# Placing every load by the plan, writing key features over the exponentials, and searching the order of a transformer block anew

## The chip, the cores and the metric

The kernel runs on one core of a Trainium2 chip. Times are device microseconds (us) of that core. Runs come in a fast and, now and then, a slow state (a lower granted TensorE clock or a time over 1.5% above the fastest of its kernel); fast runs are compared with fast runs. PE is TensorE, PEld its weight loads, DVE VectorE, ACT ScalarE, POOL GpSimd, SP the engine that issues most DMAs. "KVZ" below is the moment at which the key/value state of the linear attention is written to SBUF; S is the sum over key exponentials of one 128-token tile. Other names of tiles in the lines below: xn are normalized tokens, raw the same tokens transposed by a DMA, hT the transposed tokens after the modulation (scale and shift, the columns modA and modB); e and eq are the exponentials of keys and queries, S and Sq their sums, R and Rq the reciprocals, phik the normalized key features, va the values, pT the transposed query features, wo_sb the output weights. "Fillers" are matmuls on ones that compute nothing and stand where the plan believes PE idle.

## The reference, cut to what matters

```python
def _A_ref(x, wqkv, w_phi, wo):            # linear attention, 32 heads of 16
    q, k, v = split(x @ wqkv)
    pq, pk = q @ w_phi, k @ w_phi          # per head
    phi_q = concat([softmax(pq), softmax(-pq)]); phi_k = concat([softmax(pk), softmax(-pk)])
    kv = einsum('bhsf,bhsd->bhfd', phi_k, v); z = phi_k.sum(s)
    return (phi_q @ kv) / (phi_q @ z + 1e-06) @ wo
# 2048 tokens of 512, silu(c) @ w_mod gives shifts, scales and gates
h = layernorm(x) * (1 + ca) + sa;  x = x + ga * _A_ref(h, ...)
h = layernorm(x) * (1 + cb) + sb;  x = x + gb * ((silu(h @ w_gate) * (h @ w_up)) @ w_down)   # 1376 wide
```

All tokens' keys and values go into `kv` before the first query can be answered. So the kernel has a stage that ends with KVZ, and one of attention output and feed-forward behind it.

## The kernel before: the parts concerned

The kernel describes its work as operations, each with the engines that may do it and a duration for each, and a long list ORDER that says in which sequence a greedy plan places them: an entry divided by four is the operation, the rest is the chosen engine. Only the sequence on each engine, the tile chosen for each buffer and the filler matmuls come out of the plan; the chip then runs with semaphores.

```python
HOP = {"PE": 0.24, "DVE": 0.2, "ACT": 0.2, "POOL": 0.14, ...}     # us to another engine
...
for x in ORDER:
    o = self.ops[x // 4]; o.alt = o.alts[x % 4]; o.eng = o.alt[0].rstrip("*")
    o.start = max([o.at, free[o.eng]] + [p.end + ... for p in o.preds])
    if o.alt[0] == "DVE*":                       # takes turns with GpSimd
        o.start = max(o.start, free["POOL"])
    for b in o.news:
        t, b.slot = self.room(b, live); o.start = max(o.start, t)
    o.end = free[o.eng] = o.start + o.alt[1]
    if o.alt[0] == "DVE*":
        free["POOL"] = max(free["POOL"], o.end)
...
for o in sorted(self.ops, key=lambda o: (o.start, o.n)):
    if o.eng == "PE":
        fill(last, o, fns)                       # matmuls on ones where PE is planned idle
```

The first nine loads stood outside the plan, in a fixed sequence, and a key tile went through this (line numbers of the profile in comments):

```python
load("x0", ...); load("wk", ...); load("phi", ...); load("m0", ...); load("m2", ...)
load("x2", ...); load("wv", ...); load("x4", ...); load("wq", ...)
...
e = sb("kph", "e", [P, G, 2, 4, DH], BF16)                                       # 3 tiles
pl.op("ACT", r=[pk], w=[e], ...)                                                 # L600, exp(+), exp(-)
pl.op("DVE", r=[e], w=[Ss], us=1.14, fn=... tensor_reduce)                       # L610, S
pl.op([("DVE", 0.46, reciprocal), ("ACT", 0.52, Ln then Exp)], r=[Ss], w=[R])    # L616 or L614/L615
bphik[i] = sb("kph", "phik", [P, G, 2, 4, DH], BF16)                             # 4 tiles
pl.op("POOL", r=[e, R], w=[bphik[i]], us=1.92, fn=... tensor_tensor mult)        # L618
# query tile
pl.op([("DVE", 0.12, Rq * Sq), ("POOL", 0.15, same)], ...)                       # L659 or L660
pl.op([("POOL", 1.0, eq * Rq), ("DVE", 0.62, same)], ...)                        # L664
```

The two kinds of query product (L659, L664) were not marked `DVE*` when placed on DVE; the modulation of transposed tokens (L558) was.

The softmax here doesn't subtract the row's maximum and nothing guards it: scores larger than these inputs give would overflow.

Of the kernel before, what the change touches and what calls it, by code (L numbers as in the profile page):

```python
# [14 lines left out]
P = 128  # L15
S = 2048
# [19 lines left out]
def fm_size(m):  # L36
# [11 lines left out]
    0, 348, 4, 72, 76, 32, 352, 24, 336, 300, 324, 12, 312, 36, 28, 104, 8, 41, 20, 16, 44, 109, 88, 52, 1220, 152, 156, 56, 93, 112, 160, 164, 168,  # L48
    49, 172, 180, 60, 120, 128, 96, 124, 132, 177, 80, 116, 64, 184, 372, 68, 136, 140, 212, 100, 204, 84, 216, 260, 145, 456, 150, 188, 376, 460,
    208, 192, 196, 364, 448, 252, 201, 221, 476, 264, 256, 408, 224, 360, 484, 269, 340, 392, 368, 380, 272, 416, 452, 480, 304, 400, 234, 230, 356,  # L50
    412, 508, 244, 308, 249, 282, 278, 385, 328, 516, 344, 316, 332, 396, 236, 488, 420, 320, 388, 292, 464, 404, 712, 425, 468, 472, 284, 540, 240,
    504, 716, 492, 288, 428, 297, 512, 692, 496, 520, 728, 433, 832, 576, 684, 912, 524, 720, 536, 438, 736, 445, 500, 780, 688, 844, 772, 836, 442,
    696, 868, 840, 872, 700, 740, 784, 876, 880, 732, 529, 724, 768, 704, 804, 776, 788, 580, 532, 708, 584, 744, 748, 812, 808, 917, 800, 904, 936,
    864, 792, 753, 1216, 852, 816, 856, 1172, 860, 764, 756, 820, 849, 884, 908, 796, 888, 1080, 544, 1144, 548, 1236, 1184, 761, 824, 828, 932,
    920, 1112, 1176, 1084, 552, 1088, 925, 1240, 928, 1152, 1148, 1108, 1228, 1140, 892, 648, 1096, 1100, 1180, 1189, 1200, 1116, 1120, 1092, 1196,
    1160, 1104, 1156, 1164, 1193, 612, 1128, 1232, 1168, 556, 1132, 1244, 1404, 560, 1248, 1124, 1136, 1252, 1224, 1204, 1408, 620, 1468, 616, 1472,
    1420, 1425, 1436, 1428, 565, 1412, 1416, 1440, 1484, 1489, 1256, 1432, 1208, 588, 1500, 1452, 1492, 592, 1464, 1444, 1508, 1448, 1504, 1496,
    1457, 1460, 1476, 1516, 656, 652, 1212, 1521, 1524, 1368, 624, 568, 572, 596, 1640, 1480, 896, 628, 601, 633, 1528, 1372, 1680, 660, 944, 1692,
    1512, 664, 1376, 1644, 900, 1260, 1696, 940, 1700, 1704, 1568, 1572, 1724, 604, 637, 1684, 1676, 608, 1648, 668, 1008, 972, 1264, 1688, 1728,
    1732, 640, 948, 1736, 1880, 1884, 672, 952, 1268, 1012, 644, 1604, 1740, 1888, 1744, 957, 1892, 980, 1576, 2032, 1612, 1532, 1608, 1896, 1296,  # L60
    1748, 1016, 680, 2036, 976, 1900, 1540, 676, 960, 1304, 1752, 2040, 1044, 1536, 1756, 1760, 2044, 984, 1300, 1904, 1764, 1332, 1776, 1052, 1048,
    1768, 988, 964, 1780, 968, 1908, 1336, 2184, 993, 996, 1773, 2188, 2048, 1912, 2192, 1844, 1788, 2052, 1916, 1020, 1340, 1840, 1784, 1848, 1922,
    1824, 2056, 1024, 1029, 2336, 1804, 1832, 1932, 1000, 1792, 1936, 1924, 1852, 1808, 2196, 1796, 1928, 1812, 2060, 1004, 1800, 2064, 2340, 1820,
    1940, 2344, 2348, 2069, 1056, 1944, 1816, 2360, 1992, 1060, 1996, 2352, 1828, 1948, 2200, 1032, 2204, 2356, 1856, 2072, 1836, 2364, 1860, 2208,
    1040, 1956, 1065, 2000, 2090, 2077, 2086, 2081, 2092, 2096, 1068, 2368, 1964, 2212, 2216, 1272, 2372, 2222, 1308, 1276, 2144, 1281, 1036, 1284,
    2148, 2608, 2388, 2612, 1076, 2004, 2376, 1072, 1864, 2152, 2224, 1976, 2616, 2380, 2392, 2386, 2396, 2156, 1312, 1984, 1288, 2108, 2400, 1292,
    2404, 2237, 2242, 2234, 2408, 2100, 2128, 2229, 2620, 1972, 2632, 1980, 2416, 1960, 1317, 1988, 2244, 2624, 1868, 2628, 2136, 2296, 1968, 1380,
    2413, 2248, 2300, 2880, 1320, 2884, 2124, 1384, 2304, 2420, 1616, 1620, 2116, 1388, 2280, 2636, 2308, 2276, 1625, 2252, 1328, 1544, 2008, 2132,
    2434, 2888, 1324, 2437, 2012, 2430, 2640, 2644, 2426, 1392, 1709, 2284, 2456, 2288, 1952, 1548, 2440, 2648, 2260, 2140, 2892, 2896, 2444, 2268,
    2652, 2112, 2120, 1553, 2660, 2524, 2448, 1396, 2532, 2016, 1720, 2292, 2664, 1400, 2657, 2160, 2544, 2900, 1344, 2104, 2460, 1628, 3164, 2904,  # L70
    2548, 2668, 1636, 2020, 2672, 1348, 2164, 2024, 3168, 2464, 2168, 2676, 2680, 1632, 3172, 1580, 2552, 2556, 2492, 2908, 1584, 2686, 2472, 3696,
    2264, 2480, 2688, 1589, 2912, 1353, 1593, 2692, 2272, 2705, 2701, 2932, 1356, 2709, 1556, 2508, 2500, 2916, 1364, 2698, 2488, 2496, 2172, 1360,
    2920, 2476, 3700, 3704, 2924, 1564, 2712, 2504, 2728, 2936, 2940, 2516, 2312, 1560, 2944, 2930, 2716, 3152, 2732, 2316, 3156, 2948, 2720, 3160,
    2256, 2512, 2952, 2764, 2960, 3424, 2760, 1652, 2958, 2964, 2520, 1656, 2528, 2320, 2768, 2536, 2800, 1660, 2540, 3204, 2981, 2736, 2973, 2452,
    2484, 2977, 3428, 2324, 2772, 2560, 2564, 2968, 1873, 3000, 1665, 2984, 1600, 3432, 3208, 1596, 3176, 2568, 2748, 3212, 2572, 2744, 3216, 3220,
    1668, 2988, 2329, 2752, 3436, 2780, 1672, 2808, 3720, 3224, 2788, 2756, 3440, 2796, 3448, 2468, 3444, 3180, 3004, 3008, 3229, 2804, 3184, 2584,
    3188, 3708, 3192, 3196, 3201, 2816, 2776, 2588, 3724, 3712, 2820, 2812, 3476, 3716, 2824, 3728, 3732, 3736, 3740, 3745, 2592, 3236, 3452, 3232,
    3254, 2028, 3456, 2828, 3460, 3748, 3464, 3246, 2784, 2740, 3032, 3241, 2792, 3480, 3036, 3484, 3249, 2332, 3488, 3492, 3040, 3256, 3272, 3044,
    2856, 3752, 3260, 2596, 3756, 2724, 3276, 3468, 3496, 3760, 2860, 3473, 2832, 3764, 3504, 3768, 3264, 3501, 3280, 2864, 3508, 3521, 3088, 3772,
    2601, 3776, 3524, 3516, 2992, 3513, 3092, 2836, 2868, 1717, 3528, 3096, 3544, 3780, 3548, 3532, 3284, 2577, 2840, 2996, 3785, 2844, 3789, 3100,  # L80
    3794, 1876, 2604, 3536, 3068, 3016, 3798, 3552, 3048, 3800, 2177, 3816, 3024, 3072, 3076, 3080, 3056, 1712, 3020, 3084, 3012, 3820, 3052, 3028,
    3344, 3804, 3128, 3268, 3060, 3064, 3132, 3136, 3104, 3108, 3808, 3112, 3308, 3324, 3140, 3352, 3332, 2873, 3304, 3340, 3824, 3348, 3288, 3296,
    2180, 3145, 3328, 3356, 3292, 3300, 3336, 3316, 3360, 3312, 3364, 3320, 3368, 3372, 3376, 3380, 3384, 2580, 3400, 3404, 3408, 3412, 3417, 3540,
    3420, 2849, 3560, 3148, 3116, 3616, 3828, 3576, 3584, 3624, 3612, 3600, 3568, 3636, 2852, 3580, 3564, 3620, 3588, 3572, 3596, 3604, 3592, 3632,
    3672, 3121, 3556, 3628, 3608, 3648, 3676, 3640, 3644, 3680, 3652, 3656, 3832, 3884, 3660, 3892, 3852, 3888, 3848, 3388, 3896, 3860, 3900, 3868,
    3836, 3904, 3840, 3872, 3812, 3856, 3665, 3864, 2876, 3392, 3684, 3844, 3396, 3908, 3912, 3876, 3880, 3920, 3916, 3688, 3924, 3124, 3692, 3928,
    3932, 3937, 3944, 3948, 3952, 3956, 3668, 3940, 3961, 3964, 3968, 3972, 3976, 3980, 3984,
# [35 lines left out]
class Plan:  # L123


    HOP = {"PE": 0.24, "DVE": 0.2, "ACT": 0.2, "POOL": 0.14, "SP": 0.0, "XBAR": 0.0, "NONE": 0.0}
    OWN = {"PE": 0.0, "DVE": 0.19, "ACT": 0.19, "POOL": 0.12, "SP": 0.0, "XBAR": 0.0, "NONE": 0.0}
    DMA = (1.8, 350e3, 0.6)

    def __init__(self, slots):  # L130
        self.ops = []
        self.slots = slots
        self.queue = 0.0, 0.0
# [34 lines left out]
    def run(self, fill):  # L168
        free = {e: 0.0 for e in self.OWN}
        live = {t: {} for t in self.slots}  # L170
        free["XBAR"], dma = self.queue
        for x in ORDER:
# [4 lines left out]
            if o.alt[0] == "DVE*":  # L177
                o.start = max(o.start, free["POOL"])
            for b in o.news:
                t, b.slot = self.room(b, live)  # L180
                o.start = max(o.start, t)
# [5 lines left out]
            if o.eng == "XBAR" and o.kb > 0:  # L187
                dma = max(dma, o.start + self.DMA[0]) + o.kb * 1024 / self.DMA[1]
                o.end = max(o.end, dma + self.DMA[2])
            elif o.eng == "XBAR" and o.kb == 0:  # L190
                dma = max(dma, o.end + 0.65) + 0.5
                o.end = max(o.end, dma + 0.05)
# [10 lines left out]
def kernel(  # L203
# [72 lines left out]
    pools["modp"] = modp  # L276

    lastf = fm_size(FM - 1)
    at = {}

    def load(name, dst, src, kb):
        nc.sync.dma_start(dst, src)  # L282
        sent[0] += kb
        at[name] = 2.1 + sent[0] * 1024 / 360e3 + 1.1
# [416 lines left out]
    for c_i in (2, 3):  # L701
        later(x_ch[c_i][:], x_v[c_i], bx[c_i * TPC:(c_i + 1) * TPC], 512)
# [329 lines left out]
```

## Time and profile before

| | before |
|---|---|
| median of 3 runs (215.97 with the fourth, taken later) | 216.40 us (215.53 to 216.98) |
| profiled span | 213.3 us, clock 1.000 |
| first S, KVZ, first gate matmul of the feed-forward | 17.0, 62.6, 74.5 us |
| DVE busy in the stretch from 17.0 to 62.5 | 44.70 of 45.50 us |
| PE idle behind KVZ | 6.3 us |

The moments are read from the timelines of DVE and PE: the start of the first reduction at L610, of the product that writes KVZ (L742), and of the first matmul at L853.

### The profile page before, as it was taken

The numbers are of one execution on the slowest core, as the hardware profiler recorded it, in microseconds if no ns is written. First come the engines' busy times: TensorE is split into PE (matmuls) and PEld (weight loads), VectorE is DVE, ScalarE is ACT, GpSimd is POOL, SyncE is SP. The second block draws the span as 40 slices with busy tenths as digits, with TensorE's granted clock in tenths as the row PEclk, the third lists the DMA queues.
The fourth block names the chain that finished last, engine by engine and source line by source line (L and its number), as shares of the span: only waits on it lengthen the run. The fifth ranks groups of instructions, "written<-read, shape, count | busy, mean of one in ns | idle before, by whom it ended". The sixth has DMA issues, their size and how long they took to land.

```text
span 213.3 us, 4651 instructions
## 1 busy us (share of the span) xinstructions
PE 195.6 (92%) x1748; PEld 131.0 (61%) x1771; DVE 153.4 (72%) x301; ACT 113.5 (53%) x237; POOL 114.5 (54%) x162
## 2 busy tenths in 40 slices
PE   7899998996978999699999899999989999899993
PEld 2745553543344595588867575757668585685862
DVE  6689999999999997779897686868566202433243
ACT  2698999769896994225431615526364051320420
POOL 1249994868998465846998632266327031040350
PEclk9999999999999999999999999999999999999999
DMA  5996969793224364646444633624443000210013
GB/s 192 382 337 120 369 105 273 160 401 140 51 41 85 74 97 84 77 91 103 87 62 98 101 80 80 100 57 104 97 49 117 0 3 0 66 55 0 0 52 100
DMA packets 51241, 23.96 MB, mean 112 GB/s; under 512 B 42417, under 2 KB 48018, under 8 KB 51218
## 3 DMA queue, kind: packets, MB, share of 16 engines
q1 hardware_dynamic: 51072, 23.59, 45.8%
q8 instruction: 14, 0.23, 0.4%
q14 instruction: 9, 0.07, 0.1%
q10 hardware_dynamic: 146, 0.07, 0.1%
HBM read 11.58 MB, written 2.10 MB: 64 GB/s over the span
## 4 chain that ended last, share of the span: by engine, by line
PE 42%; DVE 22%; DMA 20%; POOL 5%; SPq 4%; issue 4%; ACT 2%; DVEq 0%; POOLq 0%; ACTq 0%
PE one_ps L853 21%; PE one_ps L924 11%; DMA pT<-eq 7%; DVE S L610 6%; DMA raw<-xn 5%; DMA wq<-in_A_wqkv_dram 4%; PE one_ps L799 4%; DVE Sq L656 3%; PE one_ps L648 3%; DVE hT L558 2%; DVE eq L664 2%; DMA out_dram<-ot 2%; SPq L282 2%; DMA WT<-wq 2%; PE kv_ps L768 1%
## 5 line engine op out<-in xcount | busy, mean ns | idle before, releaser
L853 PE MATMUL one_ps<-hT,wgu_sb 128*128 128x256 bf16 (+1 forms) x800 | 76.1, 251 | 0.8 <-DVE fg L936 0.8
L853 PEld LDWEIGHTS <-wgu_sb 128*128 128x128 bf16 x800 | 65.2, 98 | 10.4 <-issue 0.9
L860 ACT ACTIVATE sg<-one_ps 128x512 bf16<-128x512 f32 (+1 forms) x42 | 23.4, 576 | 45.0 <-PE one_ps L853 42.2
L924 PE MATMUL one_ps<-wd_sb,gu 128*128 128x512 bf16 (+2 forms) x168 | 39.0, 372 | 0.4
L869 POOL TENSOR_TENSOR gu<-usb,sg 128x512 bf16<-128x512 bf16 x16 | 19.2, 1205 | 35.8 <-ACT usb L867 24.2
L618 POOL TENSOR_TENSOR phik<-e,R 128x1024 bf16<-128x1024 bf16 x16 | 31.1, 1958 | 6.8 <-DVE R L616 3.4
L863 DVE TENSOR_TENSOR gu<-one_ps,sg 128x512 bf16<-128x512 f32 (+1 forms) x26 | 16.5, 640 | 19.8 <-PE one_ps L853 16.1
L924 PEld LDWEIGHTS <-gu 128*128 128x128 bf16 (+1 forms) x187 | 18.1, 98 | 16.5 <-DVE gu L863 0.2
L361 DVE BATCH_NORM_STATS2 st<-x_c 128x6 f32<-128x512 bf16 x32 | 21.2, 677 | 1.7 <-DMA x_c<-in_A_x_dram 1.5
L936 DVE TENSOR_TENSOR fg<-one_ps,gab 128x512 bf16<-128x512 f32 (+1 forms) x16 | 10.5, 664 | 12.3 <-PE one_ps L924 12.2
L656 DVE TENSOR_REDUCE Sq<-eq 128x64 f32<-128x1024 bf16 x16 | 19.2, 1201 | 0.0
L610 DVE TENSOR_REDUCE S<-e 128x64 f32<-128x1024 bf16 x16 | 18.9, 1184 | 0.0
L600 ACT ACTIVATE e<-one_ps 128x512 bf16<-128x512 f32 x32 | 17.3, 620 | 1.6 <-POOL phik L618 1.6
L802 DVE TENSOR_TENSOR x_c<-x_c,one_ps 128x512 bf16<-128x512 bf16 x16 | 10.9, 684 | 9.9 <-PE one_ps L799 9.9
L652 ACT ACTIVATE eq<-one_ps 128x512 bf16<-128x512 f32 x32 | 17.1, 623 | 0.6 <-PE one_ps L648 0.6
L593 PE MATMUL one_ps<-wv,hT 128*128 128x512 bf16 x63 | 15.9, 379 | 1.7 <-ACT e L600 1.0
L799 PE MATMUL one_ps<-wo_sb,oT 128*128 128x512 bf16 x57 | 15.9, 379 | 0.7 <-DMA oT<-o 0.4
L824 ACT ACTIVATE hT<-raw,modB 128x256 bf16<-128x256 bf16 (+1 forms) x17 | 8.8, 568 | 14.0 <-DMA raw<-xn 14.0
L589 PE MATMUL one_ps<-wk,hT 128*128 128x512 bf16 x59 | 15.7, 379 | 0.2
L648 PE MATMUL one_ps<-wq,hT 128*128 128x512 bf16 x63 | 15.7, 379 | 0.1
L867 ACT CAST usb<-one_ps 128x512 bf16<-128x512 f32 x16 | 9.2, 580 | 8.2 <-PE one_ps L853 8.2
L826 POOL TENSOR_SCALAR hT<-raw,modB 128x256 bf16<-128x256 bf16 (+1 forms) x12 | 6.1, 520 | 12.5 <-DMA raw<-xn 12.5
(110 smaller groups left out, 272.3 us busy)
## 6 DMA issues: line engine op xcount, KB each, us to landing
wmod_sb<-in_w_mod_dram SPq DMA_DIRECT2D x2, 1024.0 KB, 7.0
out_dram<-ot SPq DMA_DIRECT2D x15, 128.0 KB, 1.9
x_c<-in_A_x_dram SPq DMA_DIRECT2D x3, 512.0 KB, 10.6
wgu_sb<-in_B_w_gate_dram SPq DMA_DIRECT2D x1, 1376.0 KB, 8.4
wgu_sb<-in_B_w_up_dram SPq DMA_DIRECT2D x1, 1376.0 KB, 11.3
wd_sb<-in_B_w_down_dram SPq DMA_DIRECT2D x1, 1280.0 KB, 6.3
wmod_sb<-in_w_mod_dram SPq DMA_DIRECT2D x2, 512.0 KB, 5.3
x_c<-in_A_x_dram SPq DMA_DIRECT2D x2, 256.0 KB, 4.3
```

Of the source, the lines that this page charges most:

```text
L361: pl.op("DVE", r=reads, w=[st6], us=0.6, fn=lambda: nc.vector.bn_stats(st6()[:], src))
L600: nc.scalar.activation(e()[:, :, sg].rearrange("p g h f -> p g (h f)"), pk()[:].rearrange("p (g n) -> p g n", g=G), ACT.Exp, scale=(1.0, - ...
L610: pl.op("DVE", r=[e], w=[Ss], us=1.14, fn=lambda: nc.vector.tensor_reduce(Ss()[:], e()[:].rearrange("p g s h f -> p (g s h) f"), axis=AX.X ...
L618: pl.op("POOL", r=[e, R], w=[bphik[i]], us=1.92, fn=lambda: nc.gpsimd.tensor_tensor(bphik[i]()[:].rearrange("p g s h f -> p (g s h) f"), e ...
L648: nc.tensor.matmul(pq()[:], lhsT=hT[c_i][k][:, cols], rhs=Wq2[:, k, :], start=(k == 0), stop=(k == KD - 1))
L652: pl.op("ACT", r=[pq, btab], w=[be[sg]], us=0.48, fn=lambda sg=sg: nc.scalar.activation(eq[:, :, sg].rearrange("p g h f -> p g (h f)"), pq ...
L656: pl.op("DVE", r=be, w=[Sq], us=1.14, fn=lambda: nc.vector.tensor_reduce(Sq()[:].rearrange("p g s h -> p (g s h)"), eq[:].rearrange("p g s ...
L799: nc.tensor.matmul(a()[:], lhsT=oT()[:, j, :], rhs=wo_sb[:, j, :], start=(j == 0), stop=(j == KD - 1))
L853: nc.tensor.matmul(ps_()[0:fsz, q * n:(q + 1) * n], lhsT=wgu_sb[:, k, i, m * P:m * P + fsz], rhs=h2[k], start=(k == 0), stop=(k == KD - 1))
L860: pl.op("ACT", r=[g, btab], w=[sg], us=0.08 + 0.41 * L / CW, fn=lambda: nc.scalar.activation(sg()[0:fsz, 0:L], g()[0:fsz, 0:L], ACT.Silu))
L869: pl.op("POOL", r=[usb, sg], w=[gu], us=0.17 + 0.98 * L / CW, fn=lambda: nc.gpsimd.tensor_tensor(gu()[0:fsz, 0:L], usb()[0:fsz, 0:L], sg() ...
L924: nc.tensor.matmul(fp()[:], lhsT=b()[0:fsz, c0:c0 + P], rhs=wd_[0:fsz, m, wcs], start=(m == 0), stop=(m == FM - 1))
```

## The change

The intent: all loads placed by the plan, normalized key features written over the exponentials, plan corrected for GpSimd beside VectorE, order searched anew. The core of the diff (ORDER is replaced as a whole, 997 entries by 1006):

```diff
-    HOP = {..., "XBAR": 0.0, ...}          +    HOP = {..., "XBAR": 0.08, ...}
-    DMA = (1.8, 350e3, 0.6)
+    DMA = (2.1, 350e3, 0.5)
+    LANES = 8
...
+            if o.eng == "XBAR" and len(sent) >= self.LANES:
+                o.start = max(o.start, sent[-self.LANES])
...
-    slots = {..., "e": 3, "S": 3, "R": 3, "phik": 4, "va": 4, ...}
+    slots = {..., "e": 6, "S": 3, "R": 3,
+             "va": 6, ...}
...
-    load("x0", x_ch[0][:, 0:2, :], x_v[0][:, 0:2, :], 256)     (and eight more, in a fixed sequence)
+    later(x_ch[0][:, 0:2, :], x_v[0][:, 0:2, :], bx[0:2], 256)  (and ten more, as operations of the plan)
...
-        bphik[i] = sb("kph", "phik", [P, G, 2, 4, DH], BF16)
-        pl.op("POOL", r=[e, R], w=[bphik[i]], us=1.92, fn=lambda: nc.gpsimd.tensor_tensor(
-            bphik[i]()[:]..., e()[:]...,
+        bphik[i] = e
+        pl.op("POOL", r=[e, R], w=[e], us=1.92, fn=lambda: nc.gpsimd.tensor_tensor(
+            e()[:]..., e()[:]...,
...
-        pl.op([("DVE", 0.12, lambda: nc.vector.tensor_tensor(Rq()[:], Rq()[:], Sq()[:, :, 0], op=ALU.mult)),
-               ("POOL", 0.15, ...
+        pl.op([("DVE*", 0.12, lambda: nc.vector.tensor_tensor(Rq()[:], Rq()[:], Sq()[:, :, 0], op=ALU.mult)),
+               ("POOL", 0.22, ...
-        pl.op([("POOL", 1.0, lambda: fm(nc.gpsimd)), ("DVE", 0.62, lambda: fm(nc.vector))], ...
+        pl.op([("POOL", 1.02, lambda: fm(nc.gpsimd)), ("DVE*", 0.62, lambda: fm(nc.vector))], ...
```

XBAR is the plan's name for the DMA queue, and LANES lets a transfer start only when the eighth before it has ended. Nothing that is computed changes. Lines move: L610, L618, L659/L660 and L664 of before are L611, L619, L660/L661 and L665 in the new kernel (and again one less in some of the experiments, whose list is a line shorter).

## The prediction

> **What bounds the kernel now.** I read the page first, the busy rows of the 40 slices (5.33 us each), to find the stages:
>
> ```profile
> PE   7899998996978999699999899999989999899993
> PEld 2745553543344595588867575757668585685862
> DVE  6689999999999997779897686868566202433243
> ACT  2698999769896994225431615526364051320420
> POOL 1249994868998465846998632266327031040350
> ```
>
> VectorE (DVE) stands at 9 from slice 4 to slice 16, about 16 to 80 us; TensorE (PE) is full from slice 15 on. PE's 9s before that mislead: its weight-load row is half empty there, and it is padded with filler matmuls. So there are two stages: a DVE one that ends with the key/value state (KVZ), and a PE one behind it. Next, the stretches cut at the points that the timeline gives (first key-sum S at 17.0, KVZ at 62.5, first gate matmul near 75.4); columns: stretch, length, then busy time of PE, PEld, DVE, ACT, POOL:
>
> ```profile
> 0.00:17.00 17.00, 14.84 (x139) 7.98 (x140) 12.39 (x41) 11.22 (x23) 5.71 (x26) 1.00 0.93 290
> 17.00:62.50 45.50, 41.26 (x340) 21.06 (x345) 44.70 (x69) 40.57 (x90) 38.31 (x27) 1.00 0.65 189
> 62.50:75.40 12.90, 11.29 (x97) 6.44 (x99) 12.43 (x27) 10.93 (x24) 9.00 (x13) 1.00 0.44 89
> ```
>
> From 17.0 to 62.5 DVE is busy 44.7 of 45.5 us. But not all of that is work. The DVE timeline of this stretch (start, length, line, times):
>
> ```profile
> 32.41 2.75 DVE L558 TENSOR_SCALAR hT<-raw,modA 128x512 bf16<-128x512 bf16 x3 [0.21 <-DMA raw<-xn]
> ...
> 41.48 2.30 DVE L558 TENSOR_SCALAR hT<-raw,modA 128x512 bf16<-128x512 bf16 x2
> ...
> 48.30 1.30 DVE L659 TENSOR_TENSOR Rq<-Rq,Sq 128x32 f32<-128x32 f32 x1
> ...
> 51.06 1.64 DVE L664 TENSOR_TENSOR eq<-eq,Rq 128x512 bf16<-128x512 bf16 x1
> ...
> 58.90 2.20 DVE L664 TENSOR_TENSOR eq<-eq,Rq 128x512 bf16<-128x512 bf16 x1
> ...
> 62.58 0.68 DVE L742 TENSOR_TENSOR KVZ<-kv_ps,bm 128x512 bf16<-128x512 f32 x1
> ```
>
> and GpSimd (POOL) at the same times:
>
> ```profile
> 28.65 5.71 POOL L618 TENSOR_TENSOR phik<-e,R 128x1024 bf16<-128x1024 bf16 x3
> 37.75 5.88 POOL L618 TENSOR_TENSOR phik<-e,R 128x1024 bf16<-128x1024 bf16 x3 [3.39 <-DVE R L616]
> ...
> 50.23 6.24 POOL L618 TENSOR_TENSOR phik<-e,R 128x1024 bf16<-128x1024 bf16 x3 [0.68 <-PE kv_ps L625]
> 56.74 3.82 POOL L618 TENSOR_TENSOR phik<-e,R 128x1024 bf16<-128x1024 bf16 x2 [0.27 <-PE one_ps L648]
> ```
>
> Each stretched DVE instruction lies inside a run of POOL multiplies. What they cost undisturbed, from the same trace: a 128x512 tensor_scalar 0.40 us (row L405, 402 to 410 ns); L664 0.72 (five take 6.1 in all; less 1.64, 2.20 and 0.81 leaves 1.45 for two); L659 0.16 (five take 3.0; less 1.30, 0.25 and 1.14 leaves 0.31 for two). So the loss before KVZ is 5.05 - 5 x 0.40 = 3.05 (L558), 0.92 + 1.48 = 2.4 (L664), 1.14 + 0.09 = 1.23 (L659): **6.7 us on the engine that bounds**.
>
> After KVZ the PE timeline has idle pieces of 0.69, 0.38, 1.66, 0.19, 0.35, 1.25, 0.45, 0.53 and 0.76 us before 205 us, 6.3 in all out of 150.8; the list of waits names the largest part:
>
> ```profile
> PE kv_ps L768 <- DMA pT<-eq: 3.7, 4, 1.7
> ```
>
> **What the Trainium skill says.** "SBUF — State Buffer", section "Who interferes with whom": DVE and GpSimd share a pair of ports as an exclusive lock; a DVE instruction with two SBUF inputs, or a copy or tensor_scalar in a 2-port mode, blocks or is blocked for a whole instruction; tensor_reduce never is. The trace agrees: L664, L659 (two SBUF inputs) and L558 (tensor_scalar) stretch, while 16 reductions L610 stay between 1154 and 1208 ns beside busy POOL. "DMA: Bandwidth & Descriptors", section "Where 436 GB/s comes from", gives about 358 GB/s from HBM for one core. Here wk (768 KB into the queue) landed at 1.18 + 4.3 = 5.5 us and wq (3600 KB) at 4.72 + 8.67 = 13.4: 2832 KB in 7.9 us, 368 GB/s; close, and I use 368. "Trainium Kernel Development and Optimization", section "Performance Expectations", calls matmul busy time a bad metric because matmuls are pipelined. It agrees: L853 shows 251 ns each, yet 72 of them pass in 7.86 us on the chain.
>
> **The change part by part.** An entry of ORDER divided by four is the operation and the rest its engine, so I listed the operations and read both orders by engine (nine loads are new operations, so numbers shift by 11, then 9).
>
> (a) Loads. Before: x0, wk, phi, m0, m2, x2, wv, x4, wq. After: x0, x2, phi, wk, x4, m0, m2, chunk 2 of x, wq, wv. The first eight token tiles arrive early, so DVE can do eight row statistics (0.63 us each: two take 1.27) where it now stands idle: in the first 17 us it is busy 12.39, and 0.9 of the rest is the start. The price is the modulation weights: 2576 KB into the queue in place of 1808, which lands at 5.5 + (2576 - 768) x 1024 / 368e3 = 10.5 us, not 8.5. The modulation columns are then out near 11.2 (0.55 of matmuls, 0.3 of copies; now 9.3). DVE's order then has two evacuation pairs (0.72 each), four statistics of chunk 2 (3088 KB: 11.95 us by the same rule) and one more pair before the first S: 11.2 + 1.44 + 2.5 + 0.1 + 0.72 = 16.0. That is 1.0 earlier, with four more statistics done.
>
> (b) DVE between the first S and KVZ. Against 44.7 now: four statistics fewer -2.5, an evacuation pair fewer -0.7, L558 two in place of five -3 x 0.40 = -1.2, a normalization more +0.4, a va copy more +0.68, a reciprocal R more +0.5, one Sq reduction more +1.15, one reciprocal Rq fewer -0.3, one wo_sb product more +0.4 (L940's size): -1.57. Without contention: 45.5 - 6.7 - 1.6 = 37.2. The work moved off goes to ScalarE (five L558) and POOL (one L558, three normalizations at 0.77).
>
> (c) Contention. The plan now treats L659 and L664 on DVE as it already did L558: wait for POOL, hold POOL. But L558 was so marked and still lost 3.05 on five, because chip and plan drift apart. The new order has ten markable operations in the stretch (two L558, three normalizations, two L659, two L664, one wo_sb). I choose 0.5 us each, between zero and the 0.74 that nine lost now: 5 us, as a wait in the plan or on the chip. KVZ at 16.0 + 37.2 + 5 = **58.2**, so 4.3 earlier.
>
> (d) phik over e, six tiles of e in place of three plus four of phik, six va. The multiply is the same size. It frees waits of 0.7 (POOL on kv_ps) and 1.6 (ScalarE on phik) us; neither engine bounds the stretch, so alone worth nothing to 0.5 us.
>
> (e) After KVZ, PE has the same matmuls (eight query tiles lie before KVZ in both orders). Half of wo_sb is folded on DVE, but the first projection at 67.5 waits for attention and not for that. The transposes' landing is modelled anew; I allow 0.9 of the 6.3 us of gaps. The sum is 4.3 + 0.9 = 5.2 us: 216.4 - 5.2 = **211.2 us**, as the distance of the timed median from the profiled span (3.1 us) should not change.
>
> **The rivals.** (1) POOL takes over as the bound: 16 multiplies are 31.1 us, the plan runs them nearly without a break after more normalizations; from about 18 us that is 50, plus 0.8 for L558 and the DVE holds, 54. It has some 4 us of room; if the first R comes at 20 it has 2. Then KVZ stays at 60 and the time at 213 to 214. (2) ScalarE: it is busy 40.57 of 45.5 now, and all its exponentials must precede the table change at 75.25 us. Its load falls slightly by the new order (about -0.6 us), so a 4 us shorter stage leaves it near 97%. For it speaks that ScalarE waits are short already; against it that 19 query exponentials are still done after KVZ. It would halve the gain: 213 to 214. (3) The gain is given back in the PE stage, where attention waits for transposes that share one queue: more queries earlier, but the same transposes per microsecond. 1 to 3 us either way. (4) The search finds much more: gaps of the PE stage halved and contention near zero, another 5 us: 206 to 207.
>
> **Range and chances.** The contention term is 5 with 3 either way, the start 1.5, the PE stage 2; together about 3.5 either way at 8 in 10, a little more on the slow side below 215 because three rivals cost: 207.0 to 214.6. Two per cent is 212.1, only 0.9 above the middle: faster 0.61, same 0.35, slower 0.04.
>
> **What would show it.** First S near 16 (step a), KVZ near 58 (b, c), L664 and L659 on DVE under 0.9 and 0.3 us (c), first gate matmul near 71 and about 138 us from there to the end (e). It is wrong if KVZ comes after 61, if POOL shows no idle between the multiplies with DVE waiting for phik, or if PE's gaps behind KVZ grow over 8 us.

## The result, and the profile after

The new kernel took 210.32 us in the median of four runs (209.99 to 213.47; the run of 213.47 was slow, and the three fast ones have a median of 210.21), beside 215.97 for the kernel before. The ratio is 0.9734 (95% interval 0.9671 to 0.9796). A ratio here is the mean time of one kernel's fast runs over the mean of the other's fast runs of the same rounds, so not quite the ratio of the medians. The profiled span is 208.4 us, 4.9 less than before.

The busy rows of the page of the new kernel, in 40 slices of 5.21 us:

```profile
PE   7999899989999997979999999999996999999992
PEld 2664455545555896668658786587575866777741
DVE  6899979999999999579897778476444605062322
ACT  2699889989899952362415235224332450313210
POOL 3468968959986682958484953947536560042241
```

The DVE stage has the same shape, and PE's weight loads, which the prediction takes for the better sign of real work, first reach 8 or more in slice 14, at 68 us, where before they do so in slice 15, at 75. The stretches, cut at first S, KVZ and first gate matmul (the third of the prediction ran 0.9 us past its gate matmul, so the two thirds are not to be compared; stretch, length, busy time of PE, PEld, DVE, ACT, POOL):

```profile
0.00:16.60 16.60, 15.09 (x148) 8.68 (x149) 13.72 (x47) 11.24 (x26) 8.46 (x31) 1.00 0.90 315
16.60:58.50 41.90, 40.36 (x340) 20.98 (x338) 39.66 (x62) 38.65 (x85) 35.62 (x23) 1.00 0.84 204
58.50:70.00 11.50, 11.48 (x93) 6.24 (x92) 10.67 (x25) 11.13 (x25) 8.13 (x12) 1.00 0.34 69
```

First S begins at 16.63, KVZ at 58.58, the first gate matmul at 69.97 us. So 4.0 of the 4.9 us are there at KVZ, and DVE does more before the first S (13.72 us busy in 16.6, as against 12.39 in 17). The stretch between them is 3.6 us shorter. By the sums of the two traces that is 4.2 less of stretching (2.5, worked out further below, in place of the prediction's 6.7), 0.8 less of other work (37.2 in place of 38.0) and 1.4 more idle time (2.2 in place of 0.8). No run undid these parts one by one. The DVE lines that answer to the stretched ones of before, from the DVE timeline of the new kernel:

```profile
28.28 0.63 DVE L559 TENSOR_SCALAR hT<-raw,modA 128x512 bf16<-128x512 bf16 x1 [1.52 <-DMA raw<-xn]
...
29.16 0.70 DVE L559 TENSOR_SCALAR hT<-raw,modA 128x512 bf16<-128x512 bf16 x1
...
41.35 2.27 DVE L660 TENSOR_TENSOR Rq<-Rq,Sq 128x32 f32<-128x32 f32 x2
...
45.27 1.28 DVE L665 TENSOR_TENSOR eq<-eq,Rq 128x512 bf16<-128x512 bf16 x2
...
58.58 0.68 DVE L741 TENSOR_TENSOR KVZ<-kv_ps,bm 128x512 bf16<-128x512 f32 x1
```

and POOL at the same times:

```profile
26.84 1.93 POOL L619 TENSOR_TENSOR e<-e,R 128x1024 bf16<-128x1024 bf16 x1 [0.42 <-DVE R L617]
28.75 0.96 POOL L563 TENSOR_SCALAR hT<-raw,modA 128x512 bf16<-128x512 bf16 x1
32.02 11.54 POOL L619 TENSOR_TENSOR e<-e,R 128x1024 bf16<-128x1024 bf16 x6 [2.31 <-ACT R L616]
46.11 11.84 POOL L619 TENSOR_TENSOR e<-e,R 128x1024 bf16<-128x1024 bf16 x6 [2.55 <-ACT R L616]
```

The two products L665 begin in the pause that POOL has between 43.56 and 46.11, and take 0.64 us each, no more than undisturbed. They reach into POOL's next multiply, though: that one takes 2.22 us where nearly all others take 1.93. The two L660, which the plan had marked too, still lie inside a run of six multiplies and take 2.27 for what is 0.32 undisturbed; one of them alone takes 1.96, the other 0.38. POOL's last run, six multiplies without a pause, ends at 57.95; then come the last key/value matmul and KVZ. Two lines of the list of waits, for the stage behind KVZ:

```profile
PE one_ps L893 <- POOL hT L825: 3.1, 2, 1.6
...
PE kv_ps L767 <- DMA pT<-eq: 1.9, 3, 1.1
```

PE's idle pieces behind KVZ are 1.50, 1.06, 0.41, 0.44, 1.61 and 0.22, in all 5.2 us, 1.0 less than before; the largest now wait for tokens that arrive by a transposing DMA and are modulated on POOL.

### The profile page after: what moved, and what is told of

Same layout as the page of the kernel before. It is cut to its first block, busy times and chain, and to the rows that moved or that the text cites. A ratio compares the mean times of both kernels' runs of the same rounds, so it can differ in the third digit from the quotient of the medians.

```text
span 208.4 us, 4695 instructions
## 1 busy us (share of the span) xinstructions
PE 196.2 (94%) x1775; PEld 131.8 (63%) x1775; DVE 147.3 (71%) x298; ACT 108.1 (52%) x230; POOL 123.4 (59%) x173
## 4 chain that ended last, share of the span: by engine, by line
PE 48%; DMA 19%; DVE 13%; POOL 9%; SPq 5%; issue 4%; ACT 0%; POOLq 0%; DVEq 0%
PE one_ps L852 20%; PE one_ps L923 11%; DMA raw<-xn 8%; PE one_ps L649 6%; DMA x_c<-in_A_x_dram 5%; DMA pT<-eq 5%; PE one_ps L798 4%; SPq L291 4%; DVE S L611 3%; POOL gu L868 2%; PE one_ps L594 2%; PE one_ps L590 2%; POOL eq L665 2%; DVE st L350 2%; PE kv_ps L767 1%
## 5 line engine op out<-in xcount | busy, mean ns | idle before, releaser
L923 PE MATMUL one_ps<-wd_sb,gu 128*128 128x512 bf16 (+3 forms) x176 | 40.1, 372 | 0.0
L868 POOL TENSOR_TENSOR gu<-usb,sg 128x512 bf16<-128x512 bf16 x16 | 18.4, 1153 | 26.7 <-ACT sg L859 21.6
L619 POOL TENSOR_TENSOR e<-e,R 128x1024 bf16<-128x1024 bf16 x16 | 30.7, 1946 | 5.7 <-ACT R L616 5.0
L611 DVE TENSOR_REDUCE S<-e 128x64 f32<-128x1024 bf16 x16 | 18.8, 1195 | 0.0
L825 POOL TENSOR_SCALAR hT<-raw,modB 128x256 bf16<-128x256 bf16 (+1 forms) x13 | 7.2, 559 | 17.8 <-DMA raw<-xn 17.8
L823 ACT ACTIVATE hT<-raw,modB 128x256 bf16<-128x256 bf16 (+1 forms) x12 | 6.3, 559 | 20.0 <-DMA raw<-xn 20.0
L665 POOL TENSOR_TENSOR eq<-eq,Rq 128x512 bf16<-128x512 bf16 x13 | 13.7, 1056 | 1.1 <-ACT oT L787 0.7
```

Source lines behind the costliest of these rows:

```text
L611: pl.op("DVE", r=[e], w=[Ss], us=1.14, fn=lambda: nc.vector.tensor_reduce(Ss()[:], e()[:].rearrange("p g s h f -> p (g s h) f"), axis=AX.X ...
L619: pl.op("POOL", r=[e, R], w=[e], us=1.92, fn=lambda: nc.gpsimd.tensor_tensor(e()[:].rearrange("p g s h f -> p (g s h) f"), e()[:].rearrang ...
L868: pl.op("POOL", r=[usb, sg], w=[gu], us=0.17 + 0.98 * L / CW, fn=lambda: nc.gpsimd.tensor_tensor(gu()[0:fsz, 0:L], usb()[0:fsz, 0:L], sg() ...
L923: nc.tensor.matmul(fp()[:], lhsT=b()[0:fsz, c0:c0 + P], rhs=wd_[0:fsz, m, wcs], start=(m == 0), stop=(m == FM - 1))
```

## The experiments

Twelve runs were made, all on one chip; two of them repeat a kernel. Each was correct. The sequence is a list, so parts of it can be undone by themselves.

### Is it the list or the code around it?

`old_order` is the new kernel with the old list (renumbered) and the old sequence of loads:

```diff
-ORDER = [44, 0, 68, 20, ...]                 # new
+ORDER = [0, 4, 8, ..., 32, 44, 36, 48, ...]  # nine loads as before, then the old entries renumbered
```

> The new kernel's code (phik over e, six e and six va tiles, corrected constants, loads in the plan) with the old sequence of operations and of loads. Theory A (the sequence carries the whole gain, the code around it none): first S near 17, KVZ 62 to 63, time 215 to 217 us, ratio to before 0.995 to 1.005. Rival B (the freed tiles or the new fillers and slots matter by themselves): KVZ before 61 and a time under 214.

Measured: 218.74 us, ratio 1.0084 (0.9990 to 1.0177), KVZ at 63.3. That is outside the expectation, upward. KVZ is 0.3 above it; what does not fit at all is the first gate matmul, at 78.3, 15.0 us behind KVZ where the kernel before needs 11.9. The PE timeline says why:

```profile
64.07 1.89 PE L990 MATMUL kv_ps<-ones 128*128 128x512 bf16 x8
...
67.77 1.67 PE L990 MATMUL one_ps<-ones 128*128 128x512 bf16 x7
```

These are fillers. The plan, with its new constants, believed PE idle there and put fifteen of them into PE's stream in front of the attention of the first tiles; the kernel before has none behind 60.6 us, and the new kernel none behind 13.4. So a sequence-only experiment is not clean until fillers are held fixed. `old_order_f` repeats it without them:

```diff
-FILL_FROM, FILL_TO, FILL = 1.3, 90.0, 0.85
+FILL_FROM, FILL_TO, FILL = 1.3, 20.0, 0.85
```

> As old_order, but with no filler matmuls planned after 20 us (old_order had 15 of them between KVZ and the first projections, 3.2 us in TensorE's stream). Theory A (the sequence carries the gain; old_order's 218.7 was the fillers): KVZ 62.5 to 63.5, first gate matmul near 75, time 215 to 216.5, ratio to before 0.995 to 1.003. Rival (the new tiles or constants themselves cost time): still over 217.5.

Measured: 216.54 us (0.04 above the expected range), ratio 0.9991 (0.9921 to 1.0062), KVZ at 63.49, first gate matmul at 75.39, again 11.9 behind KVZ. The new tiles, the new constants and writing in place are worth nothing that these runs resolve under the old sequence. The fillers delayed the gate matmul by 3 us; at the end at most 2.2 us are theirs, because three of the four runs of `old_order`, the profiled one among them, had a granted clock of 0.982 to 0.992, and the one at 1.000 took 217.03.

### Which half of the list?

The list was cut at KVZ, and old and new halves combined (operations that the first half had already taken are dropped from the second):

```diff
+ORDER = new[:KVZ+1] + [x for x in old if x not in new[:KVZ+1]]     # new_then_old; old_then_new the other way
```

> New sequence up to KVZ, then the old sequence for all that is left. Theory A (4.0 us gained before KVZ, 1.0 behind it): KVZ at 58.6, then 150.8 us, span 209.4, time 211.3. Rival C (the second half's new sequence is what counts): time above 213.

> Old sequence (and loads) up to KVZ, then the new one. Theory A: KVZ at 62.6, then 149.8, span 212.4, time 214.3. Rival C: time below 213.

They gave 211.39 us (ratio 0.9744, 0.9676 to 0.9812; KVZ 58.83), as theory A has it, and 215.58 (0.9931, 0.9861 to 1.0002; KVZ 63.85), 1.3 above theory A, each with eight late fillers. Without them:

> As new_then_old without late fillers (it had 8, about 2 us, near 62 us). Theory A (4.0 before KVZ, 1.0 behind): KVZ 58.7, 150.5 us behind it, time 211. If the fillers cost what they measure, up to 1.5 us less: 209.8, and then the second half's new sequence is worth nothing.

> As old_then_new without late fillers (it had 8 between 66 and 68.3). Theory A: KVZ 63, 149.8 behind it, time 214 to 214.8; if the second half's new sequence is worth nothing, 215.2 to 216.

| first half, second half | median us | ratio to before | KVZ |
|---|---|---|---|
| old, old (`old_order_f`) | 216.54 | 0.9991 (0.9921 to 1.0062) | 63.49 |
| old, new (`old_then_new_f`) | 214.74 | 0.9901 (0.9840 to 0.9962) | 63.46 |
| new, old (`new_then_old_f`) | 211.50 | 0.9760 (0.9695 to 0.9825) | 59.26 |
| new, new (the new kernel; second time) | 210.32; 211.71 | 0.9734; 0.9749 | 58.58; 58.64 |

Taking out the eight fillers changed the first nothing (211.39 and 211.50) and the second 0.8 us; so what fillers cost depends on where they stand. `new_then_old_f` is 0.5 above its theory A, `old_then_new_f` inside it. Changing the first half takes off 5.0 us, the second half 1.8 after the old first half and at most 1.2 after the new one, in intervals that overlap. So the gain lies in front of KVZ; a gain of the second half is likely but not resolved.

### The loads

`loads_back` keeps every engine's sequence and only issues the first ten loads as before (the plan puts in other fillers before 17.4 us, 19 more):

```diff
-loads: x0, x2, phi, wk, x4, m0, m2, chunk 2, wq, wv
+loads: x0, wk, phi, m0, m2, x2, wv, x4, wq, chunk 2
```

> The new kernel with its first ten loads in the old sequence (x0, wk, phi, m0, m2, x2, wv, x4, wq, chunk 2), the engines' sequences unchanged. Theory A (early token tiles are part of the gain, and the new VectorE sequence depends on them): the statistics of tiles 4 to 7 wait for x4 until 12 us and hold up modA behind them, first S near 19, KVZ near 61, time 212 to 213.5. Rival (only removed contention counts): within 0.7 us of the new kernel's 210.3.

Measured: 215.02 us, ratio 0.9911 (0.9845 to 0.9978), KVZ at 61.79. The kind of mechanism is the expected one, statistics that hold up modA behind them; but the wait is for x2 and not for x4, and the size is larger. The DVE timeline:

```profile
9.05 0.69 DVE L349 BATCH_NORM_STATS2 st<-x_c 128x6 f32<-128x512 bf16 x1 [4.24 <-DMA x_c<-in_A_x_dram]
...
15.03 0.16 DVE L474 COPY modA<-one_ps 128x4 f32<-128x4 f32 x1
...
20.20 1.21 DVE L610 TENSOR_REDUCE S<-e 128x64 f32<-128x1024 bf16 x1
```

DVE stands still for 4.24 us at the third tile of its sequence, which comes with x2, and nothing passes it. What the modulation columns need from DVE (silucT, now at 11.5 and in the new kernel at 7.1) waits behind it, they come out at 15.0 (11.7 in the new kernel), and S comes at 20.2 in place of 16.6. The early token loads and the sequence that uses them are one thing; with the loads taken back, two thirds of the gain are gone by the ratios and three quarters by the profiled spans (212.1 beside 208.4 and 213.3). What the new loads would do under the old sequence was not run.

### The tiles

`own_phik` would have been the plain test: six tiles of e and four of phik. It does not fit into SBUF (found when building it, so there is no run). Nor does the plan find a tile for every operation of the new list with three, four or five of e, phik over e; it needs six of e and five of va. So the old budget (three e, four phik, four va) was given to the new list, and an operation that finds no tile waits in the list until it does; three move by more than three entries. Late fillers are off here too (FILL_TO = 20.0):

```diff
-"e": 6, "S": 3, "R": 3, "va": 6        bphik[i] = e
+"e": 3, "S": 3, "R": 3, "phik": 4, "va": 4        bphik[i] = sb("kph", "phik", ...)
+ORDER: key exponentials of tiles 2 and 7 and one va copy 5 to 7 entries later
```

> The new kernel with phik in tiles of its own again (three e, four phik, four va) and the three operations that find no tile then (two key exponential pairs, one va copy) moved five to seven entries back, no late fillers. Theory A (the tiles are worth little by themselves): KVZ under 59.5, time within 1 us of after_again. Rival (the freed tiles carry the new sequence): KVZ after 60, time over 211.5.

Measured: fast runs of 214.69 and 217.34 us (two more were slow), ratio 0.9958 (0.9896 to 1.0020), KVZ at 63.88. The rival holds. From the list of waits between 16 and 60 us:

```profile
ACT e L600 <- POOL phik L618: 6.2, 5, 2.8
POOL phik L618 <- ACT R L615: 6.2, 3, 2.4
```

ScalarE waits five times, 6.2 us in all, for POOL to give back an exponential's tile; in the new kernel's list this wait does not occur, and the second stands at 5.0. The Trainium skill, page "Perfetto Trace Analysis", section "Optimization Strategy", says that a gap which keeps coming back on the engine that should be full can mean too few tiles. Here the gap sits on ScalarE, and DVE, the full engine, gets its exponentials late: the wait of S for L600 adds up to 3.2 us. One thing blurs the size: PE waits 2.1 us at one time in this stage, and the granted clock is 0.76 from 35 to 40 us and 0.90 from 40 to 45. It is not the whole loss, for the other fast run, at a clock of 0.997, took 217.34. The run says that this sequence needs the six tiles; it does not say that no good sequence exists for the old ones.

One more thing in this run: the same pair of products (L659 here) that took 2.27 us in the new kernel took 0.22. POOL stood idle at 45.9 (DVE first, then POOL):

```profile
45.93 0.22 DVE L659 TENSOR_TENSOR Rq<-Rq,Sq 128x32 f32<-128x32 f32 x2
...
46.19 1.93 POOL L618 TENSOR_TENSOR phik<-e,R 128x1024 bf16<-128x1024 bf16 x1 [0.63 <-DVE Rq L659]
```

### The port waits

`rq_pool` takes away the largest that is left: the two L660 go to POOL, where the plan has a variant of them. Late fillers are off (FILL_TO = 20.0), but the new kernel has none behind 13.4 us either: compared without buffer numbers, the two kernels' instructions on every engine stand in the same sequence except for these two (PE compared by its weight loads, since some matmul records are missing).

```diff
-... 1252, 1144, 596, 1176, ..., 1268, 632, 1260, ...
+... 1252, 1144, 597, 1176, ..., 1268, 633, 1260, ...
```

> The new kernel with its two stretched products L660 (2.27 us on VectorE for two that take 0.16 undisturbed) on GpSimd. Theory D (VectorE with its port waits still bounds the stage): KVZ 1 to 2 us earlier, near 57, time 208.5 to 209.5. Rival E (GpSimd's chain of multiplies bounds it by now): KVZ unchanged or up to 0.6 us later, time 210 to 211.

Measured: 208.70 us, ratio 0.9628 (0.9565 to 0.9692), KVZ at 57.52. From its POOL and DVE timelines:

```profile
41.77 0.46 POOL L660 TENSOR_TENSOR Rq<-Rq,Sq 128x32 f32<-128x32 f32 x2
42.19 1.93 POOL L618 TENSOR_TENSOR e<-e,R 128x1024 bf16<-128x1024 bf16 x1
45.34 11.44 POOL L618 TENSOR_TENSOR e<-e,R 128x1024 bf16<-128x1024 bf16 x6 [1.22 <-DVE eq L664]
```

```profile
43.14 2.12 DVE L664 TENSOR_TENSOR eq<-eq,Rq 128x512 bf16<-128x512 bf16 x2
...
57.52 0.68 DVE L740 TENSOR_TENSOR KVZ<-kv_ps,bm 128x512 bf16<-128x512 f32 x1
```

2.27 us on DVE became 0.46 on POOL. Of that, 0.8 us was lost again at once: the pair L664, which had run in POOL's pause, now starts inside a multiply and takes 2.12. KVZ came 1.1 us earlier, although S had begun 0.5 later. It follows POOL's last run: that starts 0.77 us earlier than in the new kernel (45.34, not 46.11) and takes 0.40 less (11.44, not 11.84), as no DVE product reaches into it. Since this beats the new kernel, both were run again in one call:

> The new kernel unchanged, as the measure for the other runs of this call: 209.9 to 210.6 us, ratio to before 0.970 to 0.977.

> rq_pool unchanged, beside the new kernel. Theory D (the two port waits of L660 cost the end 1.0 to 1.9 us): 1.0 to 1.9 us under after_again, ratio to before 0.961 to 0.968. Rival (rq_pool's 208.7 was the chip): within 0.5 us of after_again.

`after_again` gave 211.71 us (ratio 0.9749, 0.9714 to 0.9785) and `rq_pool_again` 208.68 (0.9632, 0.9603 to 0.9660). The intervals do not touch: the kernel with two products of 32 numbers a row moved to the other engine is more than 1% faster. The new kernel came out 1.1 us above its expected range this time (the kernel before too read higher, 216.99 in place of 216.23). The 3.0 us between the medians are more than the expected 1.0 to 1.9, and more than the 1.6 between the two earlier calls. The profiled spans differ by 2.8 (209.7 and 206.9), of which 0.9 are there at KVZ (58.64 and 57.77). The remaining 1.9 come after the first gate matmul, where PE's idle pieces add up to 6.4 us in the one and 4.6 in the other, at the same instructions in the same sequence. Why they are shorter was not found, so only the 0.9 to 1.1 us at KVZ are traced to the two products.

`b_eq_pool` does the like in the kernel before, with three L659 and three L664:

```diff
-... 560, ..., 596, ..., 668 ...   565, ..., 601, ..., 637 ...
+... 561, ..., 597, ..., 669 ...   564, ..., 600, ..., 636 ...      and FILL_TO = 20.0
```

> The old kernel with its three products L659 and three L664 that lie on VectorE near KVZ put on GpSimd, no late fillers. VectorE loses 5.5 us before KVZ (1.30 + 0.36 + 1.64 + 2.20), GpSimd gains 2 x 0.25 + 2 x 1.06 = 2.6. Theory D: KVZ 1 to 2.5 us earlier, 60 to 61.5, time 213.7 to 215.2. Rival E (GpSimd's last five multiplies without a gap already set KVZ): KVZ 62.5 to 65, time 216 to 218.

Measured: 217.45 us, ratio 1.0014 (0.9973 to 1.0056), KVZ at 61.86: the time that theory E gave, and a KVZ that neither theory did. From its POOL and DVE timelines:

```profile
55.52 5.70 POOL L618 TENSOR_TENSOR phik<-e,R 128x1024 bf16<-128x1024 bf16 x3
61.18 0.25 POOL L660 TENSOR_TENSOR Rq<-Rq,Sq 128x32 f32<-128x32 f32 x1
```

```profile
61.75 0.19 DVE L740 SCALAR_TENSOR_TENSOR KVZ<-kv_ps,bm4z 128x32 bf16<-128x32 f32 x1 [1.84 <-PE kv_ps L625]
```

DVE lost its 5.4 us (the expectation's 0.36 is 0.25 in the trace) and then stood idle for 1.84 in front of KVZ, because POOL, with one L660 and one L664 more in front of it (1.3 of the 2.6 us), finished its last multiply at 61.2 (60.6 before). Behind KVZ POOL worked without a pause until 70.8 on the products and on wo_sb; PE waited 1.4 us there for transposed queries, the second query's product having begun on POOL only at 61.5, and the first gate matmul came at 75.4, as in `old_order_f`. Of 5.4 us taken from DVE nothing reached the end. In this stage DVE and POOL are near their bound together: of the two moves tried, the one that paid was small on POOL (0.46 us) and dear on DVE (2.27), and the one that put 2.6 us on POOL around KVZ did not.

## Why the prediction was right, and where not

The total was right: 211.2 us predicted, 210.3 measured, within the range, and the likeliest of the three outcomes came. By its steps:

**(a) Loads: right in kind, too large in size.** First S predicted at 16.0, measured at 16.63 (17.03 in `after_again`), so 0.3 us earlier and not 1.0; the modulation columns at 11.7 and not 11.2. The traces have ten statistics in front of the first S before and twelve after, so two more and not four. `loads_back` shows that the loads matter more than this term, since the sequence hangs on them.

**(b) and (c) The stretch from S to KVZ: the sum right, its second term for half another reason.** Predicted 37.2 + 5 = 42.2 us, measured 58.58 - 16.63 = 41.95. The work, DVE's 39.66 us less the port waits, is 37.2 as predicted, with some luck: the four statistics fewer (-2.5) were two, and the predicted 37.2 starts from the length of the stretch and so holds 0.8 us of idle time. The 5 us were to be port waits of ten instructions at 0.5. The trace has 1.95 on two L660 and 0.63 + 0.70 - 2 x 0.40 = 0.53 on two L559, so 2.5, and nothing on the others; another 2.24 are idle time of DVE (41.90 - 39.66), 1.52 of it for a transposed tile. The port waits, 6.7 us in the old kernel, came down to 2.5. Of the signs named in advance L664 (now L665) held, at 0.67 and 0.68 us; L659 (now L660) was to take under 0.3 us and takes 1.13 in the mean (0.38 and 1.96).

**(d) Tiles: the step that failed most.** "Neither engine bounds the stretch, so alone worth nothing to 0.5 us" agrees with the run of the old sequence (`old_order_f`, ratio 0.9991), and misleads: under the new one, taking the tiles back moved KVZ from 58.6 to 63.9 (`old_tiles`). The prediction weighed the tiles by the waits in the old profile (0.7 and 1.6 us), and these show what the old sequence needed, which already fits three and four tiles.

**(e) Behind KVZ: 0.9 predicted, 1.0 in the profiles (149.8 us in place of 150.8), not established.** The second profile of the same kernel has 209.7 - 58.64 = 151.1 there. The term is as large as the scatter. The first gate matmul came at 69.97, 4.5 before the true 74.48; the predicted 71 came from 75.4.

**The rivals.** POOL as the bound was judged to cost a KVZ of 60; in fact POOL and DVE now finish the stage together at 58, and `b_eq_pool` shows POOL taking over in the old kernel when it is loaded further. ScalarE, busy 38.65 of 41.90 us, did not stop the gain. The great find of the search (206 to 207) did not come, but `rq_pool` at 208.7 shows that 1.6 to 3.0 us of it were there.

## What to carry to other kernels

Look for short instructions with long durations on the engine that is full, ask what runs beside them, and try moving those that are small on the other engine; here a long run of POOL multiplies made a 0.16 us product cost 1.1 in the mean and 1.96 at worst. Judge a buffer by what sequences it admits and not by today's waits alone: here free tiles were worth nothing until the order used them, and then this order could not do without. And when a plan also emits filler work, hold that fixed before comparing sequences.

## What the Trainium skill lacked or had wrong

- "SBUF — State Buffer", section "Who interferes with whom", has the lock right as far as these runs show, and says that whoever issues first wins. It does not say how the wait shows in a profile: here it is inside the waiting instruction's own busy time, not in the idle column. L660 of 128x32 fp32 shows 2.27 us for two beside POOL's multiplies and 0.22 for the same two beside an idle POOL, and DVE counts as busy in both.
- The same section names two slowdowns as factors, but no wait in us for one instruction. In these runs a short DVE instruction beside back-to-back POOL multiplies of 1.93 us lost up to 1.8 us (L660 in the new kernel, 1.96 for 0.16), a mean of 0.74 over nine in the kernel before.
- "Perfetto Trace Analysis", section "Optimization Strategy", looks for too few tiles in gaps of the engine that should be full. With too few tiles of e the gaps stood mainly on ScalarE (6.2 us) and only half as long on the full DVE (3.2 us).
- No page found warns that filler matmuls can hold up real work behind them in PE's sequence: fifteen of them put the first gate matmul 15.0 in place of 11.9 us behind KVZ (`old_order` and `old_order_f`), and cost at most 2.2 us at the end (218.74 and 216.54).
